# A kernel of two stages on one core: a clock model in the source orders the work, loads go batch by batch, the output of batch 2 waits staged, and the search step has three VectorE operations

## The chip, the cores and the metric

The kernel runs on one NeuronCore of a Trainium2 chip. Its engines work side by side, each through its own list of instructions: TensorE (PE; PEld is its weight load), VectorE (DVE), ScalarE (ACT), GpSimd (POOL) and SyncE (SP). Here POOL issues the loads (they cast float32 to bfloat16 on the way), the gathers and the scatters, and SP issues the stores; sixteen DMA engines carry them. The metric is the time of one execution on the device in microseconds.

## What is computed

The first stage is an attention over channels. For each of 4 batches, q, k and v are 6208 rows by 256 channels; the columns of q and k are divided by their norms over the rows, a 256x256 score matrix is soft-maxed along its rows, and v is multiplied by it. The second stage takes that output as x: a score per row, the 128 rows of each batch with the highest scores, a two-layer MLP on those, and their rows of the output replaced.

```
qn = q / (norm(q, axis=1) + 1e-06);  kn = k / (norm(k, axis=1) + 1e-06)
s = kn.transpose(0, 2, 1) @ qn / tau;  a = exp(s - s.max(-1));  a /= a.sum(-1) + 1e-09
x = v @ a
scores = einsum('bsd,d->bs', x, w_gate)
for b in range(B):
    top_idx = argpartition(-scores[b], capacity)[:capacity]      # capacity = 128
    xe = x[b, top_idx];  ye = relu(xe @ w1) @ w2                 # w1 256x1024, w2 1024x256
    out[b] = x[b];  out[b, top_idx] = xe + sigmoid(scores[b, top_idx])[:, None] * ye
```

## The kernel before, in words

**Tiles.** A batch is cut into 6 chunks of 1024 rows and a remainder of 64. A chunk is one DMA per tensor: 1 MB read, 512 KB written as `q_ch`, `k_ch` or `v_ch`, with 8 rows in each of 128 partitions. So a batch has 49 "rows" of 128 tokens: 8 per chunk and one for the remainder.

**First pass (p1, lines 246 to 268).** For each row six matmuls add to two PSUM tiles: `s_ps`, the scores, and `g_ps`, whose diagonals are the squared norms. When the batch is through, `softmax_stages` (273) makes the attention matrix `a_sb` and `aw_sb`, the product of that matrix with the gate vector.

**Second pass.** T (`p2_transpose`, 353): four rows of v are transposed on PE and copied to `vt_sb` by ACT or DVE. S (`p2_score`, 369): from `vt_sb` and `aw_sb` come the scores of the tokens, in matmuls of two columns. O (`p2_out`, 408): from `vt_sb` and `a_sb` come the output rows, two to a PSUM tile (a pair here); ACT copies a pair into `stage` (429). A chunk is four pairs, and then `emit_store` (432) issues its 1 MB store on SP. A batch has 24 pairs and the one row of the remainder.

**Selection (`select_stages`, 441).** When a batch's scores are complete, DVE and PE look for a threshold that leaves 128 tokens, in 7 steps of 8 thresholds each (lines 467 to 494): compare, count along the row, sum the counts over the partitions by a matmul, move the lower end. Then the chosen tokens become indices (`idx`), and POOL gathers their rows of v (538). `mlp_stages` (544) computes the MLP, and POOL scatters the rows into the output (599). A scatter waits for all stores of its batch.

**What sets the order.** The loop from 120 to 147 writes out a list of operations: p1 of batch b, with the second pass of batch b-1 in it behind chunk 1. Selection and MLP are generators, advanced by one stage whenever the operations emitted since add up to `SLOT_US` (63, 619). The loads stand in the order in which this list needs them; `pump` (178) emits one as soon as a buffer is free and fewer than 11 are ahead. Each of POOL's DMAs also waits until the eighth before it has landed. The stores of batch 2 (called E in the source) are held back (`deferred`) until all loads are emitted, and the first of them waits for the last load but one (640 to 648). Batch 3 is L. Its second pass comes behind its first pass, and its pairs (with what is left of batch 2's) behind its selection's start.

## Time and profile before

| | us |
|---|---|
| median of 3 runs (269.4 to 270.05) | 269.94 |
| the profiled execution's own time | 268.47 |
| its span, first to last instruction | 266.5 |
| PE busy in the span | 201.2 (75%) |
| DVE busy | 128.0 (48%) |
| ACT busy | 78.6 (30%) |

The profiled execution is 1.97 us longer than its span, and 1.47 us under the median. The busy shares are averages over stages with different limits. TensorE's granted clock was 0.94 of full speed in the mean over the span. The trace also counts the traffic of the memory: 79.04 MB read and 25.95 MB written, which is 394 GB/s over the span.

### The profile page before, as it was taken

What the parts mean: (1) busy time and instruction counts of PE and PEld (TensorE: products, weight loads), DVE (VectorE), ACT (ScalarE), POOL (GpSimd) and SP (SyncE); (2) the same over time, 40 slices, a digit from 0 to 9 for tenths busy, and PEclk for the clock granted to TensorE, in tenths of its full rate; (3) what the DMA queues carried; (4) which work ended last, traced back from release to release, by engine and by line L of the source; (5) the groups of instructions that cost most, each with busy time, mean ns of one, the idle gap of its engine ahead of it and who ended that gap; (6) DMA issues with size and microseconds to landing.
All of it is one profiled execution on the core that took longest, in us unless ns stands there. A gap on an engine that the chain in (4) does not pass through costs nothing.

```text
span 266.5 us, 6018 instructions
## 1 busy us (share of the span) xinstructions
PE 201.2 (75%) x2524; PEld 174.8 (66%) x2524; DVE 128.0 (48%) x514; ACT 78.6 (30%) x146; POOL 55.9 (21%) x103
## 2 busy tenths in 40 slices
PE   0587809799974858799996778788998868777962
PEld 0476707789964746598984667687887658555841
DVE  0100001724416468623447982776497585598631
ACT  1000000147730000108770100143300184466951
POOL 7322213212100113222201014223132201000111
PEclk9999977999989799689999979999999997899998
DMA  6999999999999999999999999999999996878892
GB/s 111 215 210 214 204 215 212 215 214 254 318 312 316 313 227 215 211 214 212 305 316 316 314 278 214 222 214 211 214 214 212 222 213 192 343 298 343 366 392 91
DMA packets 17353, 65.90 MB, mean 247 GB/s; under 512 B 1968, under 2 KB 4656, under 8 KB 14256
## 3 DMA queue, kind: packets, MB, share of 16 engines
q0 software_dynamic: 13408, 39.98, 75.8%
q1 hardware_dynamic: 3920, 25.56, 23.8%
q8 instruction: 19, 0.31, 0.4%
q14 instruction: 6, 0.05, 0.0%
HBM read 79.04 MB, written 25.95 MB: 394 GB/s over the span
## 4 chain that ended last, share of the span: by engine, by line
DMA 66%; PE 15%; DVE 11%; issue 3%; ACT 3%; POOL 1%; POOLq 0%; ACTq 0%; DVEq 0%
DMA k_ch<-in_k_dram 57%; DMA v_ch<-in_v_dram 7%; PE s_ps L261 4%; PE g_ps L265 2%; PE g_ps L263 2%; PE vt_ps L360 2%; DMA out_dram<-upd,idx 2%; ACT vt_sb L364 2%; DVE cnt L473 1%; DVE junk L280 1%; DVE cmp L469 1%; PE o_ps L424 1%; POOL q_ch L170 1%; PE m_ps L312 1%; PE sc_ps L379 1%
## 5 line engine op out<-in xcount | busy, mean ns | idle before, releaser
L261 PE MATMUL s_ps<-q_ch,k_ch 128*128 128x256 bf16 x384 | 96.5, 291 | 33.1 <-DMA k_ch<-in_k_dram 32.4
L263 PE MATMUL g_ps<-q_ch 128*128 128x128 bf16 x384 | 88.4, 230 | 1.8 <-DVE nsq L280 1.7
L265 PE MATMUL g_ps<-k_ch 128*128 128x128 bf16 x384 | 88.3, 230 | 0.0
L261 PEld LDWEIGHTS <-k_ch 128*128 128x128 bf16 x384 | 39.8, 104 | 41.5 <-DMA k_ch<-in_k_dram 37.0
L429 ACT COPY stage<-o_ps 128x512 f32<-128x512 f32 x79 | 44.5, 591 | 19.2 <-PE o_ps L424 15.4
L424 PE MATMUL o_ps<-a_sb,vt_sb 128*128 128x256 bf16 (+1 forms) x322 | 47.9, 274 | 2.1 <-ACT vt_sb L364 1.3
L265 PEld LDWEIGHTS <-k_ch 128*128 128x128 bf16 x384 | 40.0, 104 | 9.1 <-issue 2.3
L366 DVE COPY vt_sb<-vt_ps 128x1024 bf16<-128x1024 bf16 (+1 forms) x39 | 24.9, 643 | 36.1 <-PE vt_ps L360 36.0
L263 PEld LDWEIGHTS <-q_ch 128*128 128x128 bf16 x384 | 39.8, 104 | 1.1 <-issue 0.8
L424 PEld LDWEIGHTS <-vt_sb 128*128 128x128 bf16 x392 | 31.3, 99 | 11.4 <-issue 6.6
L276 ACT COPY s_sb<-s_ps 128x512 f32<-128x512 f32 x4 | 2.3, 586 | 112.2 <-PE s_ps L261 112.2
L360 PE MATMUL vt_ps<-ident_b,v_ch 128*128 128x128 bf16 x384 | 29.6, 224 | 1.9 <-ACT vt_sb L364 1.2
L379 PEld LDWEIGHTS <-vt_sb 128*128 128x128 bf16 x392 | 26.6, 98 | 5.7 <-issue 2.3
L379 PE MATMUL sc_ps<-aw_sb,vt_sb 128*128 128x2 bf16 x392 | 27.2, 165 | 2.6 <-DVE aw_sb L336 2.2
L280 DVE CUSTOM_DVE_ANT_0 junk<-g_ps,ident_f 128x128 f32<-128x128 f32 x16 | 4.7, 291 | 43.6 <-PE g_ps L265 43.2
L360 PEld LDWEIGHTS <-v_ch 128*128 128x128 bf16 x384 | 23.5, 100 | 2.9 <-issue 1.9
L170 POOL DMA_DIRECT2D q_ch<-in_q_dram x24 | 13.3, 554 | 41.0 <-DMA q_ch<-in_q_dram 19.2
L170 POOL DMA_DIRECT2D k_ch<-in_k_dram x24 | 13.0, 544 | 38.5 <-DMA k_ch<-in_k_dram 14.6
L170 POOL DMA_DIRECT2D v_ch<-in_v_dram x24 | 12.9, 538 | 34.8 <-DMA k_ch<-in_k_dram 11.6
L364 ACT COPY vt_sb<-vt_ps 128x1024 bf16<-128x1024 bf16 x13 | 12.7, 1011 | 17.2 <-PE vt_ps L360 17.2
L473 DVE TENSOR_REDUCE cnt<-cmp 128x8 bf16<-128x392 bf16 x28 | 15.7, 561 | 1.0
L469 DVE TENSOR_TENSOR cmp<-sc,thr 128x392 bf16<-128x392 f32 x28 | 15.6, 558 | 0.1
(124 smaller groups left out, 183.1 us busy)
## 6 DMA issues: line engine op xcount, KB each, us to landing
out_dram<-stage SPq DMA_DIRECT2D x24, 1024.0 KB, 9.8
q_ch<-in_q_dram POOLq DMA_DIRECT2D x24, 512.0 KB, 18.4
k_ch<-in_k_dram POOLq DMA_DIRECT2D x24, 512.0 KB, 19.0
v_ch<-in_v_dram POOLq DMA_DIRECT2D x24, 512.0 KB, 14.9
w_sb<-in_moe_w_dram POOLq DMA_DIRECT2D x2, 512.0 KB, 20.0
out_dram<-stage_rem SPq DMA_DIRECT2D x4, 64.0 KB, 12.6
wg_bcast<-in_moe_w_gate_dram SPq DMA_DIRECT2D x1, 128.0 KB, 3.0
q_rem<-in_q_dram POOLq DMA_DIRECT2D x4, 32.0 KB, 22.8
```

The costliest lines, as they stand in the source:

```text
L170: ins = nc.gpsimd.dma_start(out=t, in_=view(src, b, ci))
L261: nc.tensor.matmul(s_ps[:, cc, :], lhsT=ks[:, sl], rhs=qs, start=first and cc == 0, stop=last and cc == 1)
L263: nc.tensor.matmul(g_ps[:, cc, :], lhsT=qs[:, sl], rhs=qs[:, sl], start=first and cc == 0, stop=False)
L265: nc.tensor.matmul(g_ps[:, 2 + cc, :], lhsT=ks[:, sl], rhs=ks[:, sl], start=False, stop=last and cc == 1)
L360: nc.tensor.transpose(vt_ps[:, cc, j, :parts], in_=vt[:parts, s0 + j, cc * P:(cc + 1) * P], identity=ident_b[:parts, :parts])
L364: nc.scalar.copy(vt_sb[:, :, :n, :parts], vt_ps[:, :, :n, :parts])
L366: nc.vector.tensor_copy(vt_sb[:, :, :n, :parts], vt_ps[:, :, :n, :parts])
L379: nc.tensor.matmul(sc_ps[:parts, col, :], lhsT=vt_sb[:, cc, j, :parts], rhs=aw_sb[:, cc, :], start=cc == 0 and col in (0, NCOL - 1), stop= ...
L424: nc.tensor.matmul(o_ps[:parts, pj, :], lhsT=vt_sb[:, cc, j, :parts], rhs=a_sb[:, cc, :], start=pj == 0 and cc == 0, stop=pj == m - 1 and ...
L429: nc.scalar.copy(st[:parts, s0 + pair * 2:s0 + pair * 2 + m, :], o_ps[:parts, :m, :])
L469: nc.vector.tensor_tensor(out=cmp, in0=sc[:, None, :].to_broadcast([P, NTHR, NCOL]), in1=thr[:, :, None].to_broadcast([P, NTHR, NCOL]), op ...
L473: nc.vector.tensor_reduce(out=cnt, in_=cmp, axis=AX.X, op=ALU.add)
```

## The change

The hand-written list and its slots go. In their place the source simulates the engines while it emits: a clock per engine, two DMA rings that take turns (`Rings`), and a loop that emits at each simulated moment whichever operation is ready, in the order chain stages, S, p1 or T, O. What this decides is a fixed order in the program; on the chip the engines still wait for semaphores alone.

- Loads: all of q and k of a batch, then all of its v, the remainder second in each; a load is emitted while fewer than 4 are under way by the model. The last q, k and v chunks come in two halves each.
- w1, w2 and the gate vector come over SP as float32, w1 and w2 into two `stage` buffers, and ACT casts them; the gate vector is spread over the partitions by a matmul instead of a 128 KB DMA.
- Stage buffers go from 7 to 9, `vt_sb` buffers from 22 to 14; in batch 3 the transposed v goes into freed q and k buffers.
- Pairs of batch 2 are made when PE is free before batch 3's second pass, and then only when all of batch 3's scores are done; the stores of batch 2 are held as before, the first of them behind the last v load but one.
- The search step: one comparison (threshold formed inside it), 7 matmuls that sum over partitions and columns, one reduction, one operation that moves the lower end.

```diff
-    ST_BUFS = 7
-    VT_BUFS = 22
-    EARLY = 4
-    AHEAD = 11
-    SLOT_US = [0.86, 0.86, 0.86, 1.7, 0.9]
+    ST_BUFS = 9
+    VT_BUFS = 14
+    AHEAD = 4
+    order = [0, NFULL] + list(range(1, NFULL))
...
     for b in range(B):
...
+        units += [("qk", b, ci) for ci in order] + [("v", b, ci) for ci in order]
+    split = [("qk", L, LAST), ("v", L, LAST)]
...
+    def pump():
+        rings.run(now())
+        flying[:] = [key for key in flying if rings.done.get(key, 1.0e9) > now()]
+        while nxt_unit[0] < len(units):
+            u = units[nxt_unit[0]]
+            if in_use[bucket(u)] >= limit[bucket(u)] or len(flying) >= AHEAD:
                 return
             emit_load(u)
...
+    nc.sync.dma_start(out=w1_st.rearrange("p a c -> p (a c)").rearrange("p (dc f) -> p dc f", dc=C // P),
+                      in_=moe_w1.rearrange("(dc p) f -> p dc f", p=P))
+    nc.sync.dma_start(out=w2_st, in_=moe_w2.rearrange("(p fc) d -> p fc d", p=P))
+    nc.sync.dma_start(out=wg_row, in_=moe_w_gate[None, :])
...
-    wg_bcast = const.tile([P, C], F32)
-    nc.sync.dma_start(out=wg_bcast, in_=moe_w_gate.partition_broadcast(P))
...
-            nc.vector.tensor_tensor(out=cmp, in0=sc[:, None, :].to_broadcast([P, NTHR, NCOL]),
-                                    in1=thr[:, :, None].to_broadcast([P, NTHR, NCOL]), op=ALU.is_ge)
...
-                nc.vector.tensor_reduce(out=cnt, in_=cmp, axis=AX.X, op=ALU.add)
...
-            nc.tensor.matmul(mps[:, 0:NTHR], lhsT=ones_b, rhs=cnt, start=True, stop=True)
...
+            nc.vector.scalar_tensor_tensor(out=cmp, in0=sc[:, :, None].to_broadcast([P, NCOL, NTHR]),
+                                           scalar=wl[:, i, NTHR:NTHR + 1],
+                                           in1=tab[:, None, i, :].to_broadcast([P, NCOL, NTHR]),
+                                           op0=ALU.subtract, op1=ALU.is_ge)
...
+            for h in range(7):
+                nc.tensor.matmul(mps[:, 0:7 * NTHR], lhsT=ones_b,
+                                 rhs=cmp[:, 7 * h:7 * h + 7, :].rearrange("p s j -> p (s j)"),
+                                 start=h == 0, stop=h == 6)
+            nc.vector.tensor_reduce(out=cnt9[:, 0:NTHR],
+                                    in_=mps[:, 0:7 * NTHR].rearrange("p (s j) -> p j s", s=7),
+                                    axis=AX.X, op=ALU.add)
+            gej = moe.tile([P, NTHR + 1], F32, name="gej", bufs=2)
+            nc.vector.scalar_tensor_tensor(out=gej, in0=cnt9, scalar=float(CAP) - 0.5, in1=wl[:, i, :],
+                                           op0=ALU.is_ge, op1=ALU.mult,
+                                           accum_out=wl[:, i + 1, NTHR:NTHR + 1])
...
+        if deferred and units[-2] in load_inst:
+            for b, ci in deferred:
+                st = out_store(b, ci)
...
+            if b in a_ready and (b, g) in vts and score_at > gs.index(g) + b * len(gs):
+                r = max(a_ready[b], vt_ready[(b, g)], min(o_bank))
...
+                if not acc_dead[0] or score_at == len(scores):
+                    able.append((r, 3, "O"))
```

Three places in the program show what this does to the order.

On ACT, from the start of batch 3's softmax (`s_sb`) to the first pair of the tail, before: `stage` is a pair of output rows, `vt_sb` a transposed group of v, `e` the exponential.

```order
L276 COPY s_sb<-s_ps 128x512
L429 COPY stage<-o_ps 128x512 x4
L364 COPY vt_sb<-vt_ps 128x1024
L320 ACTIVATE e,rsum<-ss_3345,rn 128x256
L320 ACTIVATE e,rsum<-ss_3348,rn 128x256
L364 COPY vt_sb<-vt_ps 128x1024 x2
L429 COPY stage<-o_ps 128x512 x2
L364 COPY vt_sb<-vt_ps 128x1024 x4
L429 COPY stage<-s_ps 128x512
L429 COPY stage<-o_ps 128x512
```

Six pairs of batch 2 stand between batch 3's softmax and its last transposes; 14 of batch 2's pairs are then done.

The same stretch after, from the last two pairs of batch 2 that come early; `q_ch` and `k_ch` now hold transposed v.

```order
L446 COPY stage<-o_ps 128x512 x2
L298 COPY s_sb<-s_ps 128x512
L393 COPY q_ch<-vt_ps 128x1024
L393 COPY q_ch<-g_ps 128x1024
L393 COPY vt_sb<-vt_ps 128x2x64
L393 COPY k_ch<-s_ps 128x1024
L342 ACTIVATE e,rsum<-e,rn 128x256 x2
L393 COPY k_ch<-vt_ps 128x1024
L393 COPY q_ch<-g_ps 128x1024
L393 COPY q_ch<-vt_ps 128x1024
L361 ACTIVATE a_sb<-e,r 128x256 x2
L446 COPY stage<-s_ps 128x512
```

Here no pair stands between the softmax and the first pair of the tail; 12 pairs and the remainder of batch 2 are done before the softmax, and 12 more of batch 2 follow with batch 3's 24.

On POOL, at the end of batch 3's loads, before: `vg` is a gather, `out_dram` a scatter.

```order
L173 DMA q_rem<-in_q_dram 64x256
L173 DMA k_rem<-in_k_dram 64x256
L170 DMA v_ch<-in_v_dram 128x2048
L599 DMA out_dram<-upd,idx 12416x256
L170 DMA v_ch<-in_v_dram 128x2048 x5
L173 DMA v_rem<-in_v_dram 64x256
L538 DMA vg<-in_v_dram,idx 128x256 x2
L599 DMA out_dram<-upd,idx 18624x256
L599 DMA out_dram<-upd,idx 24832x256
```

Both of the last gathers stand behind all loads.

The same after, from the halves of batch 3's last q and k chunk.

```order
L174 DMA q_ch<-in_q_dram 128x1024
L174 DMA k_ch<-in_k_dram 128x1024
L174 DMA q_ch<-in_q_dram 128x1024
L174 DMA k_ch<-in_k_dram 128x1024
L546 DMA vg<-in_v_dram,idx 128x256
L174 DMA v_ch<-in_v_dram 128x2048
L176 DMA v_rem<-in_v_dram 64x256
L174 DMA v_ch<-in_v_dram 128x2048 x4
L174 DMA v_ch<-in_v_dram 128x1024 x2
L546 DMA vg<-in_v_dram,idx 128x256
L608 DMA out_dram<-upd,idx 18624x256
L608 DMA out_dram<-upd,idx 24832x256
```

The gather of batch 2 now stands in front of all v loads of batch 3. The gathers of batches 0 and 1 stand likewise among the next batch's loads, in front of the last q and k chunk, and the scatters of batches 0 and 1 in front of the next batch's last v chunk.

On DVE, one step of the search before (`thr` are the thresholds, `lo` the lower end).

```order
L469 TENSOR_TENSOR cmp<-sc,thr 128x392
L473 TENSOR_REDUCE cnt<-cmp 128x8
L479 TENSOR_SCALAR base<-iota_row,steps,lo 128x8
L486 TENSOR_SCALAR ge,kk<-m_ps 128x8
L490 SCALAR_TENSOR_TENSOR thr<-kk,steps,base 128x8
L493 TENSOR_SCALAR lo<-kk,steps,lo 128x1
```

Six operations, of which `base` and `lo` are not waited for by the next comparison.

The last step after, and what follows it (`cnt` and the number are the counts, `wl` holds the lower ends and the step widths).

```order
L483 SCALAR_TENSOR_TENSOR cmp<-sc,wl,tab 128x392
L501 TENSOR_REDUCE cnt_157<-m_ps 128x8
L505 SCALAR_TENSOR_TENSOR gej,wl<-cnt_157,wl 128x9
L512 SCALAR_TENSOR_TENSOR msk,own_b<-sc,wl,slack 128x49
L516 SCALAR_TENSOR_TENSOR pre<-ones_col,msk 128x49
L518 MEMSET pre 128x1
L526 TENSOR_SCALAR oh<-iota_row,m_ps 128x128
L527 SCALAR_TENSOR_TENSOR oh<-iota_row,m_ps,oh 128x128
```

Three operations a step, each waiting for the one before it or for PE.

## Rows read from the trace of the kernel before

**Rows 1.** The page's forty slices: DMA's busy tenths
```profile
DMA  6999999999999999999999999999999996878892
```

**Rows 2.** Stretches: us, busy us of PE, PEld, DVE, ACT, POOL; PEclk, DMA share, GB/s
```profile
0.00:3.00 3.00, 0.00 (x0) 0.00 (x0) 0.00 (x0) 1.28 (x1) 1.86 (x7) 1.00 0.33 45
...
3.00:221.50 218.50, 169.25 (x2173) 149.41 (x2174) 102.77 (x415) 52.33 (x99) 50.13 (x93) 0.94 1.06 240
...
221.50:224.00 2.50, 2.50 (x45) 2.50 (x43) 1.12 (x5) 1.01 (x1) 1.00 (x1) 0.50 0.29 52
...
224.00:232.00 8.00, 5.98 (x110) 5.25 (x108) 3.71 (x13) 3.04 (x3) 0.00 (x0) 0.93 1.01 396
...
232.00:234.00 2.00, 2.00 (x12) 1.37 (x11) 1.90 (x7) 1.35 (x3) 0.00 (x0) 0.50 0.08 33
...
234.00:248.00 14.00, 10.07 (x87) 7.68 (x85) 12.58 (x54) 10.04 (x20) 0.00 (x0) 0.99 0.79 322
...
221.50:261.20 39.70, 31.29 (x350) 25.13 (x347) 24.72 (x99) 25.02 (x46) 2.96 (x3) 0.92 0.84 331
...
261.20:266.50 5.30, 0.64 (x6) 0.31 (x4) 0.48 (x1) 0.00 (x0) 0.97 (x1) 0.86 0.07 26
```

**Rows 3.** Timeline of the store queue SP: start us, us, instruction, count
```profile
0.81 0.38 SPq L217 DMA_DIRECT2D wg_bcast<-in_moe_w_gate_dram  x1
...
223.63 16.00 SPq L435 DMA_DIRECT2D out_dram<-stage  x6
```

**Rows 4.** Timeline of DVE: batch 3's selection, first and last instruction and two comparisons
```profile
229.71 0.26 DVE L446 TENSOR_REDUCE sc<-sc_ps 128x48 f32<-128x96 f32 x1 [1.04 <-PE sc_ps L379]
...
234.39 0.56 DVE L469 TENSOR_TENSOR cmp<-sc,thr 128x392 bf16<-128x392 f32 x1
...
236.34 0.55 DVE L469 TENSOR_TENSOR cmp<-sc,thr 128x392 bf16<-128x392 f32 x1
...
249.27 0.15 DVE L535 TENSOR_SCALAR idx<-fl 128x1 int32<-128x1 f32 x1
```

**Rows 5.** Timeline of POOL, which issues loads, gathers and scatters
```profile
1.34 0.72 POOL L170 DMA_DIRECT2D q_ch<-in_q_dram  x1 [0.83 <-POOLq L747]
...
250.18 0.97 POOL L538 DMA_INDIRECT vg<-in_v_dram,idx  x1 [26.90 <-PE g_ps L424]
...
262.74 0.97 POOL L599 DMA_INDIRECT out_dram<-upd,idx  x1 [4.40 <-DVE upd L593]
```

**Rows 6.** Two of the page's costliest groups: instruction, count, busy us, mean ns, idle before
```profile
L364 ACT COPY vt_sb<-vt_ps 128x1024 bf16<-128x1024 bf16 x13 | 12.7, 1011 | 17.2 <-PE vt_ps L360 17.2
...
L473 DVE TENSOR_REDUCE cnt<-cmp 128x8 bf16<-128x392 bf16 x28 | 15.7, 561 | 1.0
```

**Rows 7.** Chain of waits that ended last: one group of scores, one of transposes
```profile
220.69 0.18 PE sc_ps L379 x8
220.87 0.88 PE vt_ps L360 x8
```

**Rows 8.** Timeline of PE in the tail: two pairs of output rows
```profile
246.59 0.60 PE L424 MATMUL s_ps<-a_sb,vt_sb 128*128 128x256 bf16 x4
247.03 0.60 PE L424 MATMUL o_ps<-a_sb,vt_sb 128*128 128x256 bf16 x4
```

**Rows 9.** One more stretch, columns as in Rows 2: TensorE nearly idle
```profile
35.00:40.00 5.00, 0.08 (x1) 0.08 (x2) 0.00 (x0) 0.00 (x0) 1.06 (x2) 0.63 1.09 211
```

**Rows 10.** DMA issues from 207 us on: count, median us from issue to landing
```profile
vg<-in_v_dram,idx POOLq DMA_INDIRECT x2, 4.6
```

**Rows 11.** Timeline of the last MLP: its first PE and its last DVE instruction
```profile
256.81 0.28 PE L549 MATMUL vt_ps<-ident_b,vg 128*128 128x128 bf16 x2
...
261.88 0.48 DVE L593 SCALAR_TENSOR_TENSOR upd<-o_ps,gate,xe 128x256 f32<-128x256 f32 x1 [1.58 <-PE o_ps L590]
```

**Rows 12.** Waits of POOL: who waited for whom, total us, times, longest
```profile
POOL out_dram L599 <- DVE cnt L473: 4.9, 1, 4.9
...
POOL vg L538 <- DVE ss L319: 2.5, 1, 2.5
```

More of the change, by code (lines that the diff above doesn't have):

```diff
@@ L140 @@
[L140 to L153 removed]
+    gs = [g for ci in order for g in groups(ci)]
@@ L175, in emit_load @@
         loaded[u] = tiles
         load_inst[u] = ins
-    def pump(most=1000):
-        while state["next"] < len(units) and most > 0:
-            u = units[state["next"]]
-            bk = bucket(u[0], u[2])
-            if state[bk] >= limit[bk] or ahead[0] >= AHEAD:
+    def pump():
[4 more added lines that the diff above has]
+            if in_use[bucket(u)] >= limit[bucket(u)] or len(flying) >= AHEAD:
@@ L248, in p1_steps, with p1_row @@
+    acc = {}
+    acc_free = [0.0]
+    a_tiles = {}
+    a_ready = {}
+    aw_ready = {}
+    sc_tiles = {}
+    held = {b: len(order) for b in range(B)}
+    stored = {b: [] for b in range(B)}
+    stage_of = {}
+    stage_keys = ["w1", "w2"]
+    stage_free = {"w1": 12.0, "w2": 14.0}
+    deferred = []
+    gate_done = []
+    vts = {}
+    vt_ready = {}
+    gathered = set()
+    def p1_row(b, ci, s):
         if b not in acc:
@@ new lines, in select_stages @@
+        msk = moe.tile([P, NCOL], BF16, name="msk")
+        own_b = moe.tile([P, 1], BF16, name="own_b")
+        with nc.allow_low_precision(reason="counts of at most 49 are whole in bf16"):
+            nc.vector.scalar_tensor_tensor(out=msk, in0=sc, scalar=wl[:, NSTEP, NTHR:NTHR + 1],
+                                           in1=slack.to_broadcast([P, NCOL]), op0=ALU.subtract,
+                                           op1=ALU.is_ge, accum_out=own_b)
+        pre = moe.tile([P, NCOL + 1], BF16, name="pre")
@@ L542, in select_stages @@
-        waiting.append(b)
-    def mlp_stages(b):
-        vg, idx, _ = gathered[b]
+        vt_clock["pool"] = max(vt_clock["pool"], now()) + 1.0
+        rings.add(0, vt_clock["pool"] + 1.0, 0.5, ("gather", b))
+        gathered.add(b)
+        yield ("dma", ("gather", b))
         a_sb, _ = a_tiles[b]
@@ L710 @@
[L710 to L730 removed]
+                self.need = None
@@ new lines, in step, with ready @@
+                return
+            if y[0] == "pe":
+                vt_clock["pe"] = t0 + y[1]
+                vt_clock["dve"] = max(vt_clock["dve"], now() + 0.2) + y[2]
+                self.need = ("t", vt_clock["dve"] + 0.05)
+            else:
+                self.need = y
+        def ready(self):
+            if self.need[0] == "t":
+                return self.need[1]
+            if self.need[0] == "dma":
+                if self.b < L and not calm():
+                    return FAR
+                return rings.landing(self.need[1]) + 0.1
+            b = self.need[1]
+            if held[b] or (b >= E and L not in gathered):
+                return FAR
+            if b >= E:
+                return now()
+            return max(rings.landing(key) for key in stored[b]) + 1.0
@@ new lines @@
+    chains = []
+    eat = []
+    for u in units:
+        if u[0] == "qk":
+            eat += [("p1", u, s) for s in range(RPP if u[2] < NFULL else 1)]
+        else:
+            eat += [("T", u, g) for g in groups(u[2])]
+    eat_at = 0
+    scores = [(b, g) for b in range(B) for g in gs]
+    score_at = 0
+    outs = [(b, g, pr) for b in range(B) for g in gs for pr in range((g[2] + 1) // 2)]
+    out_at = 0
+    vt_live = 0
+    vt_bank = [0.0, 0.0]
+    o_bank = [0.0, 0.0]
+    cast_done = False
```

781 lines of the change are left out of this document (410 added, 371 removed).

## The prediction

> **What bounds the kernel now.** I read the page's forty slices first. DMA stands at nine tenths or more in 32 of them in a row, and loses tenths only in the first slice and from the 34th on [rows 1]. PE, the busiest engine, has 201.2 of 266.5 us. So I cut the span into stretches by what DMA does [rows 2]. From 3.0 to 221.5 us its share is 1.06 (packets overlap a little, so a full queue reads slightly above 1). There is nothing to win in those 218.5 us: all loads and the stores of batches 0 and 1 pass in them, and the change moves the same bytes. What can be won lies at both ends.
>
> In the first 3.0 us the share is 0.33, about 2.0 us lost. From 221.5, when the loads are over, to 261.2, when the last store is out, DMA moves 331 GB/s x 39.7 us = 13.14 MB. In the full stretch from 224 to 232 it moves 396, and I count with that: 33.2 us of work in 39.7, 6.5 us lost. They lie in three holes: 2.5 us at 0.29, 2.0 us at 0.08, 14 us at 0.79 [rows 2]. The first is there because SP's first held store starts at 223.63, two microseconds after the loads [rows 3]; it waits for the last load but one, which before is a full chunk with only the 64-row remainder behind it. The other two are there because pairs of output rows are missing: 14 pairs of batch 2 are ready, 3.5 chunks, and DMA takes 1.05 MB / 396 GB/s = 2.65 us for a chunk; the next pair is made when batch 3's scores are complete, at 229.7 [rows 4], 8.2 us after the last load. From 261.2 to 266.5 stands the last scatter, issued at 262.74 after POOL had waited 4.40 us for `upd` [rows 5].
>
> **The change part by part.**
>
> *Stores behind the loads.* In the new order the last v chunk comes in two halves, and the held stores wait for the chunk before it, so the first store starts before the loads are over: the first hole goes. Ready by then are 12 pairs and the remainder, 3 chunks or 8 us of stores. T and S of batch 3 no longer stand behind its softmax and batch 2's pairs in one block: its q and k are in 15 us before its last v, so when the last half chunk lands only one group of T and S remains: 0.88 for the transposes at the lower clock, 1.01 for ACT's copy, 0.18 for the scores [rows 6, 7], 2.1 us. A chunk of four pairs is then ready about 4 us after the last load, and DMA needs it after some 7. From there on, the order puts three pairs between two search steps. A pair takes 0.44 us on PE, from start to start [rows 8], three take 1.32, and a step about 1.8 (below): 2.4 us for a chunk against DMA's 2.65. So DMA should not run dry again: -6.5 us. The bounds are 0 (both holes come back) and -6.5.
>
> *The end.* The last scatter waits for `upd` before. If stores no longer starve they end about when `upd` is there; the scatter itself, 262.74 to 266.5, stays. Bounds 0 and -1.0 (262.74 less 261.2 and half a microsecond for a landing); I take -0.5.
>
> *The start.* w1 goes out on SP where the gate vector's load stood at 0.81 us, POOL's first load at 1.34 [rows 3, 5], and 2 MB on a second queue lie beside the first chunks. Bounds 0 and -2.0 (the whole loss); I take -0.7, nearest to the 0.53 between those two rows.
>
> *Weights.* The 128 KB broadcast of the gate vector goes: 0.13 MB at the body's 240 GB/s [rows 2] is -0.5. w1 and w2 are written as float32, twice 1.05 MB at the store's 2.65 us, in place of twice 0.52 MB at a load's 211 GB/s [rows 9], 2.5 us each: +0.3. ACT's casts of them have no row here; ACT is idle until the first softmax and PE does not need w1 before the first MLP, so nothing. If that cover were gone, they would cost ACT about four times its copy of 128x1024, 4 us [rows 6].
>
> *The search step.* Between two comparisons lie 1.95 us before (234.39 to 236.34), and from the first reduction to `idx` 19.7 us [rows 4]. The count over the columns, 0.56 us [rows 6], goes to PE as seven matmuls instead of one. They are not in the trace: from below seven at the eighth part of a score group's 0.18, and one group's time for the way through, 0.35 us; from above seven whole groups, 1.3 [rows 7]. I take 0.35, since matmuls in a row are pipelined there. A step is then the longer of three pairs (1.32) and DVE's part (comparison 0.56, reduction from PSUM 0.26 [rows 4], moving the end as much again, 0.2 estimated for handing over: 1.3), plus 0.35 and 0.1: 1.8 us, 1.0 us less over seven steps. In the body this is hidden by DMA. In the tail the chain runs from the last load: 2.1 to the scores, 18.7 to `idx`, 0.8 to the gather [rows 4, 5], 4.6 to its landing [rows 10], 5.6 for the MLP [rows 11], 4.1 from there to the end: 35.9 us. The stores need 33.2 less the 1 us they start earlier, and 4.8 for the end: 37.0. So the stores set the end, by 1.1 us, and the step itself is worth 0.
>
> *Loads.* Four more DMAs (the halves) cost POOL at most 0.72 each [rows 5], under DMA at 1.06. AHEAD 4 for 11 changes where gathers stand, not how early a load may go. I take 0; the other end is a rival below.
>
> Sum: -6.5 - 0.5 - 0.7 - 0.5 + 0.3 = -7.9. The span becomes 258.6, the profiled execution 268.47 - 7.9 = 260.6, and against the median, 1.47 us above the profiled execution, 269.94 - 7.9 = **262.0 us**.
>
> A rule of the Trainium skill speaks against the largest term. The page "DMA: Bandwidth & Descriptors", section "Where 436 GB/s comes from", says that between HBM and SBUF the memory's share of one core binds, about 358 GB/s. By it the 13.14 MB would take 36.7 us, only 3.0 of the 39.7 could be won, and the sum would be -4.4, 265.5 us. The trace has 396 GB/s over 8 us of stores [rows 2], so the measurement decides here.
>
> **The rivals.**
>
> *The chain sets the end.* It is 1.1 us from doing so. If PE runs the tail at its lower level, 1.2 GHz, a pair takes 0.88, a step 2.64 + 0.7 = 3.3, a chunk 4.4 us against DMA's 2.65. For this speaks that PE was granted 0.50 in 221.5 to 224 and in 232 to 234, though it was busy throughout [rows 2]; and that before the new tail it waits for one v chunk after another. Against it: in the busy stretch from 234 to 248 it had 0.99. Four steps of seven at the lower level cost 4 x 1.5 = 6.0, 4.9 after the 1.1 to spare: 266.9 us. Seven count matmuls at their upper bound, 0.95 more a step, come to nearly the same. The Trainium skill's page "TensorE: Matmul & The Clock Gate", section "Part 1: The HAM clock gate", has the half rate as the state to which an idle PE falls back until activity lifts it; by that rule the new tail opens slow, and the trace agrees as far as that the clock was 0.63 in the 5 us in which PE did almost nothing [rows 9].
>
> *Slower: POOL stands at a gather while the queue of loads runs dry.* POOL works in order. The gather of batch 2 now stands in front of all v loads of batch 3, behind its q and k loads alone, and at that time no stores are there to fill in, since they are held. Batches 0 and 1 have gathers and scatters among the next batch's loads too: five places. The cover at the gather is the q and k of the next batch, 12 x 2.5 = 30 us from the last v load, against the 2.1 + 18.7 us of the selection. The selection shares PE with p1 rows that wait for loads, and may take half as long again, 30 us; beyond that each microsecond of DMA is lost. 4 us at three of the places is 12 us: 274.0 us. It decides from 7.9 us in all. Against it: in the kernel before, POOL waited 4.9 us at one scatter in the body [rows 12], and DMA stayed at 1.06.
>
> *The holes stay.* If the transposes of batch 3 wait for their copies (1.01 us each on ACT) until after the last load as before, its scores are late again, no pair comes, and 6.5 is not won: 268.5; with 1 us lost in the body 269.5. The order speaks against it: T and S stand ahead of all pairs.
>
> **How the numbers follow.** The forecast has 0.62, with 258 to 265 as its own range (the bounds of the end and the start downward, half of the holes coming back upward); the chain at the end 0.17; the dry queue 0.11; the holes that stay 0.06; and 0.04 is left for less than 258. A measurement here can tell 0.3% from no change, that is 269.1 and 270.75. Faster: 0.62 + 0.17 + 0.04 and 0.01 of the holes, 0.84; the same 0.05; slower 0.11. The range from 257 to 269.5 leaves out the dry queue and a little of the rest on both sides.
>
> **What would show it.** DMA's share stays at 1.0 or above from 3 us to the last store, with no slice under 0.9 behind the loads; SP's first held store starts before the last v load has landed; from the last load to the end it is 37 us instead of 45; a step lies under 1.9 us. The forecast is wrong if POOL waits for `idx` while the share falls below 1 in the body, if ACT has no pair to copy in the first 8 us after the last load, or if TensorE's clock stands at 0.5 behind it.

## The result, and the profile after

The changed kernel takes 266.41 us (median of 19 runs, 263.66 to 269.88), the kernel before, run beside it, 269.55 us (19 runs, 268.37 to 270.12). The ratio is 0.9842, 95% interval 0.982 to 0.9865: some 4.3 us faster, where 7.9 were forecast. Seven of the 19 runs, the profiled one (268.82 us, span 267.1) among them, ran at a lower mean granted clock (0.876 to 0.902, the others 0.900 to 0.939) and longer; the ratio goes by the other twelve, 265.0 us in the median, and the tail is read beside that of experiment 2, which differs in one condition. The median of 266.41 lies within the whole range of the forecast (257 to 269.5), beyond the 258 to 265 of its likeliest case and near the rival in which the chain sets the end (266.9).

DMA's busy tenths on the page of the changed kernel, in forty slices, answer to [rows 1]:

```profile
DMA  6999999999999999999999999999999999599940
```

The run of nines goes one slice further than before and is broken once, in the slice that is a 5. The stretches (columns as in [rows 2]: us, busy us of PE, PEld, DVE, ACT, POOL; PEclk, DMA share, GB/s) show where:

```profile
0.00:3.00 3.00, 0.00 (x0) 0.00 (x0) 0.00 (x0) 1.28 (x1) 1.86 (x7) 1.00 0.28 48
3.00:221.50 218.50, 179.18 (x2367) 158.35 (x2367) 71.90 (x318) 80.23 (x137) 51.49 (x96) 0.93 1.06 245
221.50:224.00 2.50, 2.26 (x34) 2.26 (x35) 1.59 (x4) 0.00 (x0) 0.00 (x0) 0.50 1.05 410
224.00:227.00 3.00, 2.40 (x43) 2.32 (x40) 1.96 (x4) 0.00 (x0) 0.00 (x0) 0.50 1.01 399
227.00:229.00 2.00, 2.00 (x17) 1.50 (x18) 0.81 (x4) 0.59 (x1) 0.00 (x0) 0.50 1.04 438
229.00:232.00 3.00, 3.00 (x18) 2.33 (x17) 1.50 (x6) 1.86 (x4) 0.00 (x0) 0.58 0.13 55
232.00:252.00 20.00, 17.03 (x198) 13.44 (x196) 10.18 (x46) 17.56 (x37) 1.00 (x1) 1.00 0.99 398
252.00:256.50 4.50, 2.57 (x14) 1.89 (x15) 0.52 (x3) 0.59 (x1) 0.00 (x0) 0.50 0.33 134
256.50:260.00 3.50, 2.30 (x17) 1.60 (x16) 1.49 (x5) 0.37 (x1) 1.01 (x1) 0.50 0.85 337
```

The first hole of [rows 2] is gone: 221.5 to 229 is full. The second is there again, 3 us at 0.13, and a new one stands at 252 to 256.5. Between them DMA moves 398 GB/s over 20 us. The clock is 0.50 to 0.58 from 221.5 to 232, though PE works nearly throughout.

Four timelines of the changed kernel, SP, DVE, POOL and PE (start us, us, instruction, count, idle before and what ended it), in this order, answer to [rows 3], [rows 4], [rows 5] and [rows 11]:

```profile
220.69 0.33 SPq L451 DMA_DIRECT2D out_dram<-stage  x1
```

```profile
227.46 0.24 DVE L463 TENSOR_REDUCE sc<-sc_ps 128x48 f32<-128x96 f32 x1
...
233.41 0.63 DVE L483 SCALAR_TENSOR_TENSOR cmp<-sc,wl,tab 128x392 bf16<-128x392 f32 x1
...
234.95 0.63 DVE L483 SCALAR_TENSOR_TENSOR cmp<-sc,wl,tab 128x392 bf16<-128x392 f32 x1
...
245.44 0.15 DVE L542 TENSOR_SCALAR idx<-tok 128x1 int32<-128x1 f32 x1
...
262.52 0.48 DVE L604 SCALAR_TENSOR_TENSOR upd<-g_ps,gate,xe 128x256 f32<-128x256 f32 x1 [0.76 <-PE g_ps L599]
```

```profile
245.86 1.00 POOL L546 DMA_INDIRECT vg<-in_v_dram,idx  x1 [36.90 <-DMA out_dram<-stage]
...
263.28 0.97 POOL L608 DMA_INDIRECT out_dram<-upd,idx  x1 [4.58 <-DVE upd L604]
```

```profile
253.93 0.40 PE L556 MATMUL vt_ps<-ident_b,vg 128*128 128x128 bf16 x2 [4.23 <-DMA vg<-in_v_dram,idx]
...
254.97 1.91 PE L599 MATMUL o_ps<-w_sb,h_sb 128*128 128x256 bf16 x8
256.68 0.63 PE L562 MATMUL m_ps<-a_sb,vgt 128*128 128x256 bf16 x2
```

The first held store starts at 220.69 instead of 223.63. The scores are complete at 227.46 instead of 229.71, a step takes 1.54 us instead of 1.95 (233.41 to 234.95), and `idx` comes at 245.44 instead of 249.27. Then the gain melts: the gather is issued 4.3 us sooner than before, but its rows are used 8.1 us later (253.93) where [rows 5] and [rows 11] have 6.6, `upd` starts 8.6 us behind that instead of 5.1, and the last scatter starts at 263.28, half a microsecond later than before. The last two rows show one reason. Between the transposes of the gathered rows (253.93) and the next product on them (256.68) PE makes the last pair and the last product of batch 2's MLP (254.97, eight matmuls); in the kernel before that product comes ahead of the last gather's transposes.

### The profile page after: what moved, and what is told of

It reads as the page before. It is cut to its first block, busy times and chain, and to the rows that moved or that the text cites. A ratio compares the mean times of both kernels' runs of the same rounds, so it can differ in the third digit from the quotient of the medians.

```text
span 267.1 us, 6315 instructions
## 1 busy us (share of the span) xinstructions
PE 213.2 (80%) x2710; PEld 185.1 (69%) x2710; DVE 91.3 (34%) x390; ACT 103.2 (39%) x183; POOL 56.3 (21%) x105
## 4 chain that ended last, share of the span: by engine, by line
DMA 41%; PE 29%; issue 20%; DVE 5%; ACT 2%; POOLq 1%; POOL 0%; DVEq 0%
DMA vg<-in_v_dram,idx 12%; DMA q_ch<-in_q_dram 10%; DMA k_ch<-in_k_dram 10%; PE s_ps L288 7%; DMA v_ch<-in_v_dram 6%; PE o_ps L443 4%; PE g_ps L290 3%; PE g_ps L292 3%; PE vt_ps L381 3%; PE sc_ps L409 2%; DMA out_dram<-stage 2%; DVE junk L302 1%; ACT stage L446 1%; PE s_ps L443 1%; DMA out_dram<-upd,idx 1%
## 5 line engine op out<-in xcount | busy, mean ns | idle before, releaser
L288 PE MATMUL s_ps<-q_ch,k_ch 128*128 128x256 bf16 x384 | 93.2, 285 | 25.8 <-DMA k_ch<-in_k_dram 25.8
L288 PEld LDWEIGHTS <-k_ch 128*128 128x128 bf16 x384 | 39.2, 102 | 27.6 <-DMA k_ch<-in_k_dram 26.7
L292 PEld LDWEIGHTS <-k_ch 128*128 128x128 bf16 x384 | 39.3, 102 | 6.1
L443 PE MATMUL o_ps<-a_sb,vt_sb 128*128 128x256 bf16 (+1 forms) x270 | 41.6, 289 | 2.3 <-ACT stage L446 1.9
L443 PEld LDWEIGHTS <-vt_sb 128*128 128x128 bf16 (+1 forms) x296 | 28.9, 105 | 9.8 <-issue 4.8
L381 PEld LDWEIGHTS <-v_ch 128*128 128x128 bf16 x384 | 27.7, 111 | 11.0 <-issue 8.8
L393 ACT COPY vt_sb<-vt_ps 128x1024 bf16<-128x1024 bf16 (+1 forms) x25 | 20.9, 894 | 1.8 <-PE vt_ps L381 1.8
L546 POOL DMA_INDIRECT vg<-in_v_dram,idx x4 | 4.0, 1006 | 83.0 <-DVE idx L542 46.1
L174 POOL DMA_DIRECT2D q_ch<-in_q_dram x25 | 13.8, 553 | 32.5 <-PE g_ps L292 10.6
L483 DVE SCALAR_TENSOR_TENSOR cmp<-sc,wl,tab 128x392 bf16<-128x392 f32 x28 | 17.5, 626 | 1.0
L395 DVE COPY vt_sb<-vt_ps 128x1024 bf16<-128x1024 bf16 x15 | 10.2, 691 | 17.3 <-PE vt_ps L381 17.3
L501 DVE TENSOR_REDUCE cnt<-m_ps 128x8 f32<-128x56 f32 x28 | 6.1, 217 | 19.2 <-PE m_ps L498 19.2
```

The costliest lines, as they stand in the source:

```text
L174: ins = nc.gpsimd.dma_start(out=t[:, rows, :], in_=view(src, b, ci)[:, rows, :])
L288: nc.tensor.matmul(s_ps[:, cc, :], lhsT=ks[:, sl], rhs=qs, start=begin and cc == 0, stop=end and cc == 1)
L292: nc.tensor.matmul(g_ps[:, 2 + cc, :], lhsT=ks[:, sl], rhs=ks[:, sl], start=False, stop=end and cc == 1)
L381: nc.tensor.transpose(vt_ps[:, cc, j, :parts], in_=vt[:parts, s0 + j, cc * P:(cc + 1) * P], identity=ident_b[:parts, :parts])
L393: nc.scalar.copy(vt_sb[:, :, :n, :parts], vt_ps[:, :, :n, :parts])
L395: nc.vector.tensor_copy(vt_sb[:, :, :n, :parts], vt_ps[:, :, :n, :parts])
```

## The experiments

There are twelve. All stand beside runs of the kernel before on the same chip; the ratios are to those.

**1. The changed kernel once more.** 

> The changed kernel, not altered, as the common base of the next three. Its fast runs so far lie between 263.7 and 267.2 us, 265.1 in the mean. Clock theory (TensorE runs at 1.2 GHz in much of the tail, and how much differs from run to run): the clock is again about 0.5 from 222 to 231 us and after 252, and slower runs have the lower mean clock. Gather theory (the last gather lands late because it shares the DMA engines with stores): the last gather again takes 6 to 8 us from issue to use, whatever the clock.

Measured: 266.87 us, ratio 0.9886 (0.9846 to 0.9926); the size holds. In its trace (269.68 us) the clock is at 0.50 from 223 to 233 and again from 254 on, and the gather is used 7.7 us after its issue.

**2. All pairs ahead of the last gather's use.** In the changed kernel the last pair stands on PE behind the gather's transposes, and the store of the last chunk with it.

```diff
             if self.need[0] == "dma":
                 if self.b < L and not calm():
                     return FAR
+                if self.b == L and out_at < len(outs):
+                    return FAR
```

> The last pair of output rows stands in front of the last gather's first use on PE instead of behind it. If the stores set the end (they run dry for 3.5 us because that pair is late): 3 us less, about 262. If the chain of gather and MLP sets the end (the pair only delays it by 0.85 us): 0.5 to 1 us less, about 264.4, and the last store is out 3 us before the last scatter.

Measured: 265.05 us, ratio 0.9854 (0.9831 to 0.9877) against 0.9886 for the changed kernel in the same runs; the intervals overlap. Timelines of this kernel, DVE, POOL and PE:

```profile
227.69 0.24 DVE L463 TENSOR_REDUCE sc<-sc_ps 128x48 f32<-128x96 f32 x1
...
243.74 0.15 DVE L542 TENSOR_SCALAR idx<-tok 128x1 int32<-128x1 f32 x1
...
251.87 0.29 DVE L558 COPY vgt<-vt_ps 128x256 bf16<-128x256 bf16 x1 [5.43 <-PE vt_ps L556]
...
258.40 0.48 DVE L604 SCALAR_TENSOR_TENSOR upd<-g_ps,gate,xe 128x256 f32<-128x256 f32 x1 [0.87 <-PE g_ps L599]
```

```profile
244.17 1.00 POOL L546 DMA_INDIRECT vg<-in_v_dram,idx  x1 [34.95 <-DMA out_dram<-stage]
...
259.17 0.97 POOL L608 DMA_INDIRECT out_dram<-upd,idx  x1 [4.65 <-DVE upd L604]
```

```profile
251.54 0.29 PE L556 MATMUL vt_ps<-ident_b,vg 128*128 128x128 bf16 x2 [3.10 <-DMA vg<-in_v_dram,idx]
```

Its stretches, columns as above:

```profile
224.00:227.00 3.00, 2.62 (x49) 2.52 (x47) 1.91 (x3) 0.00 (x0) 0.00 (x0) 0.61 1.00 393
...
229.00:232.00 3.00, 3.00 (x34) 2.58 (x32) 2.62 (x12) 2.99 (x7) 0.00 (x0) 1.00 0.56 235
232.00:252.00 20.00, 16.23 (x187) 12.70 (x186) 9.15 (x40) 16.34 (x35) 1.00 (x1) 1.00 1.02 411
...
256.50:260.00 3.50, 1.86 (x9) 0.80 (x8) 1.40 (x4) 0.00 (x0) 0.83 (x1) 0.50 0.00 0
```

DMA has nothing to move from 256.5 on, but the scatter waits for `upd` until 259.17. So the stores do not set the end here; the chain does, by about 3 us. It takes 40.3 us from the last packet of a load (222.7 in the trace) to the end of the span: 5.0 to the scores, 16.1 to `idx`, 0.4 to the gather, 7.7 until its rows are copied on DVE, 7.3 to the scatter, 3.8 to the end. The forecast had 35.9.

**3. The same, and PE kept busy before the last MLP**, with 14 matmuls of 512 columns into a bank that nothing reads.

```diff
+        if b == L:
+            spare = out_psum().rearrange("p a c -> p (a c)")
+            for _ in range(14):
+                nc.tensor.matmul(spare, lhsT=ident_b, rhs=w1_sb[:, 0, 0:512], start=True, stop=True)
         mps = ps_m.tile([P, 512], F32, name="m_ps")
```

> As e1_pair_first, and 14 matmuls of 512 columns that nobody reads keep PE busy while it waits for the last gather (14 x 0.22 us = 3.1 us at 2.4 GHz). Clock theory: the last MLP, 8.6 us from gather to update at 1.2 GHz, falls to about the 5.6 us of the kernel before: 3 us less than e1_pair_first, about 261.5. If the MLP's length is not the clock's, no change against e1_pair_first, or up to 1 us more because the matmuls stand in the way.

Measured: 265.42 us (262.95 to 267.38), ratio 0.9856 (0.9811 to 0.9901): no gain that shows in the time. In the trace the clock is 1.00 from 250 to 260, where experiment 2 has 0.68, and `upd` starts 5.3 us after the copy of the gathered rows, in experiment 2 6.5 us. The clock costs the last MLP about 1.2 us, less than these runs differ among themselves.

**4. The changed kernel with PE kept busy among batch 3's transposes**, two such matmuls ahead of each of the 13 groups.

```diff
...
+        if acc_dead[0]:
+            if not spare:
+                spare.append(ps_o.tile([P, 2, C], F32, name="o_ps").rearrange("p a c -> p (a c)"))
+            for _ in range(2):
+                nc.tensor.matmul(spare[0], lhsT=ident_b, rhs=w1_sb[:, 0, 0:512], start=True, stop=True)
         for j in range(n):
```

> Two matmuls of 512 columns that nobody reads stand before each of batch 3's 13 transposes (26 x 0.22 = 5.7 us of PE at 2.4 GHz). Clock theory: the clock stays up from 213 us on, the scores are complete 2 us earlier, a pair takes 0.44 instead of 0.85, the hole of 3 us in the stores behind 229 us closes: 2 to 3 us less, about 262.5, with less spread. Late-softmax theory (PE has too much to do in batch 3's first pass, so everything behind is late whatever the clock): the added work makes it later, 0 to 3 us more.

Measured: 266.94 us, ratio 0.9918 (0.9886 to 0.9951). The clock is 1.00 from 212 to 232, and the scores are still complete at 227.69 only. That does not clear the clock: the two added matmuls take 0.43 us a group, and a group at the upper level saves about as much (0.87 to 0.44). The experiment may have cancelled what it was to show.

**5. The old search step in the kernel of experiment 2.**

```diff
...
-            nc.vector.scalar_tensor_tensor(out=cmp, in0=sc[:, :, None].to_broadcast([P, NCOL, NTHR]), ...
+            nc.vector.tensor_tensor(out=cmp, in0=sc[:, None, :].to_broadcast([P, NTHR, NCOL]), ...
+                nc.vector.tensor_reduce(out=cnt, in_=cmp, axis=AX.X, op=ALU.add)
...
-            for h in range(7):
...
+            nc.tensor.matmul(mps[:, 0:NTHR], lhsT=ones_b, rhs=cnt, start=True, stop=True)
...
```

> The kernel with all pairs ahead of the last gather's use (265.05 us, last measured), with the search step of before in it: six VectorE operations and one count matmul instead of three and seven. The step takes 1.95 us in the trace of before and 1.54 after. Theory A, the chain from the last load sets the end: seven steps cost 7 x 0.41 = 2.9 us, time 268, and idx is 2.9 us later. Theory B, the stores set the end as forecast: the step is hidden, 265.0.

Measured: 268.09 us, ratio 0.9932 (0.9898 to 0.9966), where experiment 2 had 0.9854: 0.0078, 2.1 us lost, with intervals that do not meet. Timeline of DVE:

```profile
227.40 0.24 DVE L463 TENSOR_REDUCE sc<-sc_ps 128x48 f32<-128x96 f32 x1
...
231.98 0.56 DVE L484 TENSOR_TENSOR cmp<-sc,thr 128x392 bf16<-128x392 f32 x1
...
233.93 0.56 DVE L484 TENSOR_TENSOR cmp<-sc,thr 128x392 bf16<-128x392 f32 x1
...
246.44 0.15 DVE L543 TENSOR_SCALAR idx<-tok 128x1 int32<-128x1 f32 x1
```

The step is 1.95 again, from the scores to `idx` 19.0 us instead of 16.1. Theory A holds in this order: the step is on the path that sets the end.

**6. The new search step alone in the kernel before**, with its order, loads and stores.

```diff
...
-            nc.vector.tensor_tensor(out=cmp, in0=sc[:, None, :].to_broadcast([P, NTHR, NCOL]), ...
+            nc.vector.scalar_tensor_tensor(out=cmp, in0=sc[:, :, None].to_broadcast([P, NCOL, NTHR]), ...
...
```

> The kernel before, with nothing but the new search step in it (three VectorE operations and seven count matmuls); order, loads and stores as before. Theory A, the chain from the last load sets the end in the kernel before too: seven steps of about 1.55 in place of 1.95 us take 2.8 us off, 266.7. Theory B, as forecast, the stores and their holes set the end there and the step alone is worth at most the 1.0 us between the last store and the scatter: 268.5 to 269.5.

Measured: 268.58 us, ratio 0.995 (0.9921 to 0.9979), 1.35 us faster (0.6 to 2.1 by the interval). That is the fast edge of theory B's range, and theory A's 266.7 lies outside the interval: in the order of the kernel before, the step is worth something, but not its whole 2.8 us. In the trace `idx` comes at 248.22, only 1.05 us sooner than in [rows 4], since the scores were 0.5 later (230.24) and the first two steps still took 2.34 and 1.94 us at a low clock. Even that is lost again behind it, where the rows of the gather, issued at 249.14, are copied 7.6 us later, in the kernel before 6.95. The scatter starts no sooner than in [rows 5]:

```profile
262.99 0.98 POOL L605 DMA_INDIRECT out_dram<-upd,idx  x1 [5.69 <-DVE upd L599]
```

**7. The output of batch 2 stored as soon as it is staged**, in the changed kernel.

```diff
...
-                if b >= E and not gate_done:
-                    deferred.append((b, g[0]))
-                else:
-                    out_store(b, g[0])
+                out_store(b, g[0])
```

> The changed kernel, but the output of batch 2 is stored as soon as it is staged. Theory A, what counts is when the last load lands, since the chain from there sets the end: 3.2 MB of stores go in front of the loads' end, the loads are over some 6 to 8 us later, and the time is as much longer, about 273. Theory B, DMA's bytes set the end: only their order changes, 266.9.

Measured: 277.45 us, ratio 1.0281 (1.0225 to 1.0336), 7.6 us slower than the kernel before. Stretches, and then the scores on DVE's timeline:

```profile
221.50:232.00 10.50, 7.49 (x76) 6.15 (x76) 3.87 (x20) 4.81 (x7) 1.06 (x2) 0.75 1.07 214
232.00:250.00 18.00, 15.43 (x208) 12.72 (x208) 8.53 (x34) 10.74 (x21) 0.00 (x0) 0.72 0.41 111
```

```profile
241.93 0.24 DVE L463 TENSOR_REDUCE sc<-sc_ps 128x48 f32<-128x96 f32 x1
```

The loads go on to 232 and beyond, the scores come 14 us late, and DMA, whose reserve of stores is spent, stands at 0.41 for 18 us. Theory A holds, and its size was too small: without the hold the emitted order changes as well, and more of batch 2's pairs are made and stored before the loads are over than the 3.2 MB that it counted: from 190 us to the last load's landing (233) SP's queue moves 5.8 MB in this trace, 0.5 MB in that of experiment 2 (to 223). How the 10.6 us to the changed kernel divide between the two was not tried.

**8. PE kept busy only where it waits for batch 3's softmax**, with 8 unread matmuls, on the kernel of experiment 2.

```diff
+            if b == L and g == gs[0]:
+                spare = ps_o.tile([P, 2, C], F32, name="o_ps").rearrange("p a c -> p (a c)")
+                for _ in range(8):
+                    nc.tensor.matmul(spare, lhsT=ident_b, rhs=w1_sb[:, 0, 0:512], start=True, stop=True)
             p2_score(b, g)
```

> The kernel with all pairs ahead of the last gather's use, and 8 matmuls of 512 columns into a bank that nothing reads, placed only where PE waits for batch 3's softmax in front of its first scores (1.8 us idle there). Theory A, the scores are late because PE runs its last seven transposed groups and scores at 1.2 GHz, and it does so because it idled just before: the clock stays at 1.00 in 222 to 227, 16 transposes take about 1 instead of 1.87 us, the scores are complete at about 224.5 instead of 227.7, 262. Theory B, the clock falls all the same or the scores wait for landings and copies: scores at 227.7, 265.

Measured: 266.17 us, ratio 0.9843 (0.9796 to 0.9891). The start of batch 3's scores in the timeline of PE, in experiment 2 and then in this kernel:

```profile
218.67 0.49 PE L409 MATMUL sc_ps<-aw_sb,q_ch 128*128 128x2 bf16 x14 [1.78 <-DVE aw_sb L356]
```

```profile
220.58 0.54 PE L409 MATMUL sc_ps<-aw_sb,q_ch 128*128 128x2 bf16 x16
```

The clock held at 1.00 in 222 to 227, and from the first scores to the last (227.73) PE took 7.1 us instead of the 9.0 of experiment 2 (218.67 to 227.69). But it began 1.9 us later: the softmax was 1.1 us late in this execution, and the added matmuls ran on into the scores. So between these two traces the clock is worth about 1.9 us there, and the later start took them away again; its expectation of 262 fell. No experiment that held the clock up shows a gain in the time.

**9. Sixteen transposes moved ahead of the first scores**, on the kernel of experiment 2.

```diff
-            if b in aw_ready and (b, g) in vts:
+            if b in aw_ready and (b, g) in vts and (b < L or sum(key[0] == L for key in vts) >= 9):
```

> The kernel with all pairs ahead of the last gather's use; batch 3's scores may start only when eight of its twelve full groups of v are transposed, so 16 transposes more stand in the 1.8 us in which PE waits for the softmax, ahead of the first scores, instead of behind them. Theory A, the scores are late because PE comes to the last groups late: they are complete up to 1.9 us sooner (16 transposes at 1.2 GHz), at about 226, and the end follows, 263.3. Theory B, landings and copies decide: scores at 227.7, 265.

Measured: 266.24 us, ratio 0.9849 (0.9803 to 0.9896): nothing. A timeline row of PE:

```profile
218.25 0.62 PE L381 MATMUL vt_ps<-ident_b,v_ch 128*128 128x128 bf16 x8 [0.87 <-DMA v_ch<-in_v_dram]
```

The moved transposes waited 0.87 us for their v chunk and 0.78 for a copy (at 219.66), so PE's hole could not take them; the clock was 0.50 behind it, and the scores came at 227.44. Theory A falls.

**10. The last two stores behind the last gather's landing**, on the kernel of experiment 2.

```diff
...
+        if L in g_inst and not g_gate:
+            g_gate.append(1)
+            tc.add_manual_dep(st.ins, g_inst[L].ins.name, ...
```

> The kernel with all pairs ahead of the last gather's use, and its last two stores (1 MB each) start only when the last gather has landed. Theory A, the 7.7 us from the gather's issue to its use are the stores that are queued ahead of it and beside it: it lands some 2 us sooner, the scatter follows as much sooner, 263; the two stores are late by some 3 us and still end before the scatter. Theory B, the gather takes its 7.7 us by itself: it lands no sooner, and the stores behind it end at about 258, 265 to 267.

Measured: 264.1 us, ratio 0.979 (0.974 to 0.984). **11. The last three stores so**, one of them made before the gather is issued:

```diff
...
+                if b == L and g[0] >= 3 and L not in g_inst:
+                    late.append((b, g[0]))
...
```

> The kernel with all pairs ahead of the last gather's use; its last three stores, one of them made before the gather is issued, start only when the last gather has landed. Theory A, the gather queues behind the stores issued before it: with 1 MB less ahead of it, 2.5 us at 410 GB/s, its first packet comes about 2 instead of 4.5 us after the issue and it is used after about 5.5 instead of 7.7 us; the three stores then end at about 256 to 257 and the scatter waits for them, 263 to 264.5. Theory B, the wait is the gather's own: first packet 4.5 us after the issue, used after 7.7, and the time 266 or more, since three stores come behind it.

Measured: 264.63 us, ratio 0.9797 (0.976 to 0.9834). **12. Three stores behind the gather's issue** instead of its landing:

```diff
...
+            flag = moe.tile([P, 1], F32, name="flag")
+            g_inst[b] = nc.gpsimd.memset(flag, 0.0)
...
```

> The kernel with three stores behind the last gather, but they wait for the gather's issue (a POOL memset of one column behind it) and not for its landing. Theory A, the gather waits for what is queued before it and not for what comes behind: it is still used about 5 us after its issue, and DMA's hole of some 3 us in 246 to 249 goes, so that the stores, which set the end there, are over some 2.5 us sooner: 262. Theory B, stores beside the gather slow it as much as those ahead: it is used after 7 us or more, and the chain sets the end again, 264 to 265.

Measured: 264.46 us (262.4 to 266.68), ratio 0.9793 (0.9749 to 0.9837). The timelines of POOL and DVE of these three kernels in turn: the gather, and the copy of its rows (for the first kernel the first reduction of the scores too, for the third the scatter).

```profile
242.39 1.00 POOL L548 DMA_INDIRECT vg<-in_v_dram,idx  x1 [33.67 <-DMA out_dram<-stage]
```

```profile
225.93 0.24 DVE L465 TENSOR_REDUCE sc<-sc_ps 128x48 f32<-128x96 f32 x1
...
250.10 0.29 DVE L561 COPY vgt<-vt_ps 128x256 bf16<-128x256 bf16 x1 [5.43 <-PE vt_ps L559]
```

```profile
242.75 1.00 POOL L548 DMA_INDIRECT vg<-in_v_dram,idx  x1 [33.73 <-DMA out_dram<-stage]
```

```profile
247.54 0.29 DVE L561 COPY vgt<-vt_ps 128x256 bf16<-128x256 bf16 x1 [2.52 <-PE vt_ps L559]
```

```profile
244.79 1.00 POOL L548 DMA_INDIRECT vg<-in_v_dram,idx  x1 [35.52 <-DMA out_dram<-stage]
...
258.20 0.97 POOL L614 DMA_INDIRECT out_dram<-upd,idx  x1 [6.33 <-DMA out_dram<-upd,idx]
```

```profile
249.21 0.29 DVE L564 COPY vgt<-vt_ps 128x256 bf16<-128x256 bf16 x1 [2.15 <-PE vt_ps L562]
```

From issue to use it is 7.7 us in the first, as in experiment 2, though the two stores behind it were held: its first packet still came 4.6 us after the issue. With one store less ahead of it that is 1.85 us, and it is used after 4.8. With the stores let go at its issue it is 1.9 and 4.4. So the gather waits for the stores that are queued when it is issued; a slowing by those behind it does not show. (In the traces of experiments 4, 5, 8 and 9, with the order of experiment 2 or of the changed kernel, it was used after 8.5 to 8.9.) Of theory A in experiment 10 only that half holds, and the 2 us that it expected from the other half did not come; whether its better time than experiment 2's is more than the clock in front of that (scores at 225.93 in its trace, at 227.69 in experiment 2's, where the programs do not yet differ) stays open.

DMA's stretches around the gather, first with the stores behind its landing, then behind its issue:

```profile
246.00:249.00 3.00, 2.40 (x23) 1.68 (x20) 1.09 (x5) 1.88 (x5) 0.00 (x0) 1.00 0.22 71
```

```profile
246.00:249.00 3.00, 2.83 (x36) 2.38 (x35) 0.64 (x3) 2.97 (x8) 0.00 (x0) 1.00 0.91 300
```

The hole goes (0.22 to 0.91), as expected. The time did not follow to 262: in this trace the scores were complete at 228.32 only, and the scatter, at 258.20, waited for the scatter of batch 2, not for `upd` (255.04). These three are the fastest versions of the study, about 2% under the kernel before; against the changed kernel's 0.9842 their gain is half a per cent, and the intervals overlap.

## Why the prediction was right or wrong

*Direction: right. Cause: wrong in the main.* The step that failed is the sentence "So the stores set the end, by 1.1 us, and the step itself is worth 0". The chain sets the end, by about 3 us in experiment 2; the old step in it costs 2.1 us (experiment 5), and the new step alone gives the kernel before 1.35 us (experiment 6). So in these two orders the step that was priced at nothing gives a third to a half of what the whole change gives (4.3 us); in the changed kernel's own order the old step was not tried. The trace of experiment 2 beside that of the kernel before shows the places, 3.5 us in all. It wins 2.0 us at the scores, where batch 3's transposes no longer stand among pairs of batch 2, 3.5 in the search and 0.5 to the gather's issue; it loses 0.75 until the gathered rows are copied and 1.7 from there to the scatter. The filling of DMA's holes, which was to give 6.5, is not shown to have given anything. That the time still fell into the range is owed to the range's width, which took in a rival, and not to the sum.

*The chain, 35.9 us, was mis-sized in three terms, and starts later than was thought.* The forecast set the loads' end at 221.5; the last packet of a load starts at 222.7. Scores: 2.1 us from the last landing, measured 4.8 (the profile after) and 5.0 (experiment 2), and 3.3 in the quickest trace (experiment 10). One group was to remain when the last half chunk lands; from the first scores on PE still has six groups to transpose, one after another, with a copy and scores each. At the upper clock level that takes 7.1 us, mostly at the lower 9.0 (experiment 8). Experiments 2 and 10 are one program up to there, and with the clock at 0.61 in 224 to 227 the scores came at 227.69, with 1.00 at 225.93. Experiment 10's stretches:

```profile
224.00:227.00 3.00, 2.50 (x46) 2.18 (x43) 2.07 (x7) 0.69 (x2) 0.00 (x0) 1.00 1.01 399
229.00:232.00 3.00, 3.00 (x39) 2.52 (x37) 2.37 (x12) 2.99 (x7) 0.00 (x0) 1.00 0.97 407
```

Of these 1.8 us, 0.65 are an earlier softmax and 1.1 PE's pace. So of the 2.9 us that this term missed in experiment 2, 1 to 2 are the clock by these pairs of traces, and the rest is put down to PE's order. Gather: 4.6 us, taken from a median over one gather with an empty queue and one under load [rows 10]; measured 7.4 (experiment 2) and 8.1 (the profile after) to the first PE instruction on the rows, behind a queue of stores. The term should have been 6.6, the time between the rows 250.18 and 256.81 that stood in the same tail. MLP, from the first PE instruction on the gathered rows to the end of `upd`: 5.6 us, measured 7.3 (experiment 2) and 9.1 (the profile after). The clock is a part of it: PE stood idle while the gather landed, the clock was at 0.50 behind that, and with it held at 1.00 the same stretch takes 6.1 (experiment 3). The other part is PE's order, with batch 2's last product, and in the profile after the last pair too, between the transposes and the next product on the rows: 2.75 us from the one to the other in the profile after (253.93 to 256.68), 1.0 in experiment 2, 0.7 in the kernel before. Batch 2's product ahead of the transposes again was not tried. The search itself was better than forecast, 1.54 us a step and 16.1 to 18.0 in all instead of 18.7.

*Stores behind the loads, -6.5.* The mechanism was right in its first part, and experiment 7 shows how much hangs on it. The second hole, 229 to 232, came back, because the scores were late (ACT had no pair to copy for 7.4 us) and pairs at the lower clock level come 0.85 us apart. In experiments 2 and 4, with the clock at 1.00 in the hole but the scores at 227.69, DMA's share there is 0.56; in experiment 10, with the scores at 225.93, it is 0.97. The last store is out at 259.3 instead of 261.3 in the profile after, and at 255.9 in experiment 2, so the term is -2.0 to -5.4, and the end did not follow it.

*The end, -0.5: 0.* The scatter waits for `upd` as before, and from its start to the end of the span it is 3.8 us in the profile after and in experiment 2 as before.

*Start, broadcast and weights, -0.9 together: about 0.* The share in the first 3 us is 0.28, before 0.33 [rows 2], and in both kernels the loads run dry at nearly the same time (the last packet of a load ends at 223.2 before and at 222.8 after), as one stretch of a microsecond shows, in the kernel before and in the changed one:

```profile
220.00:221.00 1.00, 0.70 (x20) 0.69 (x20) 0.46 (x4) 0.76 (x2) 0.00 (x0) 0.83 0.73 136
```

```profile
220.00:221.00 1.00, 1.00 (x29) 0.99 (x26) 0.01 (x1) 0.88 (x3) 0.00 (x0) 1.00 0.76 139
```

*Loads, 0: right.* The rival of the dry queue did not happen, though POOL stood at one gather for 18.5 us. Timeline of POOL of the changed kernel, and a stretch, the 5 us before it went on:

```profile
79.53 1.02 POOL L546 DMA_INDIRECT vg<-in_v_dram,idx  x1 [18.51 <-DVE idx L542]
```

```profile
75.00:80.00 5.00, 4.42 (x45) 3.19 (x44) 2.24 (x13) 4.29 (x9) 0.47 (x1) 1.00 1.04 318
```

After 18.5 us of waiting DMA is still at 1.04, fed by the loads issued before and by the stores of the batch before.

*The rivals and the signs.* "The chain sets the end" is what happened, near its time of 266.9, but only in part by its mechanism: the steps ran at 1.54 us with the clock at 1.00 from 232 on, and the low clock struck before them, and behind them in the MLP. That its time was near is luck. Its chance of 0.17 was too low, since 1.1 us of slack was less than the error of most terms of the chain. The two slower cases did not come. Of the forecast's own signs of being wrong, one came in full, the clock at 0.5 behind the last load, and one nearly: ACT had its first pair 6.8 us after the 221.5, where 8 was the sign.

## What to carry to other kernels

When two paths end within a microsecond or two of each other, price every operation on both; a term is worth nothing only if its path has more slack than the terms have error. A small dependent DMA waits for what stands in the queues when it is issued, so a few large stores held back until it is issued shorten its wait, and let go right behind it they leave DMA no hole; in the time that showed as about half a per cent, within the noise. A transfer that fills a gap is a reserve: here, output held back until the loads are over was worth more than output written early. Work of another batch that the emitted order puts between two links of the last chain lengthens it.

## What the hardware showed that was not expected

- A gather of 128 rows is used 7.7 us after its issue behind queued stores (experiments 2 and 10), 4.8 and 4.4 us with one MB less ahead of it (experiments 11 and 12), and the stores behind it make no difference that shows. The Trainium skill's page "DMA: Bandwidth & Descriptors", section "Queues, rings and completion order", has each engine take turns between queues, packet by packet; by that alone a gather on POOL's queue would not wait for all that is queued on SP's. The first packet's 4.6 against 1.9 us says that here it does wait.
- TensorE's granted clock stood at 1.2 GHz (0.50) for some 10 us from 221.5 on in the profile after, while PE was busy for 9.7 of 10.5 us, at first with transposes of 128 columns and scores of 2; with matmuls of 512 columns among them it stayed at 1.00 (experiment 4). Shortly ahead of the fall PE had stood idle for 0.7 us, waiting for the softmax, and with that wait filled (experiment 8) the clock stayed at 1.00 too; so no run tells whether the idle or the short matmuls lowered it. In two programs that are the same up to there it was 0.61 in one execution and 1.00 in the other (experiments 2 and 10).
- DMA moves 398 and 411 GB/s over 20 us of stores (232 to 252 in the profile after and in experiment 2), above the 358 that the Trainium skill's page "DMA: Bandwidth & Descriptors", section "Where 436 GB/s comes from", states for one core between HBM and SBUF.
